# Wider gate tiles in the first unit, a shifted PSUM ring and an earlier request for x

## The chip, the core and the metric

The kernel runs on one core of a Trainium2 chip. The metric is the device time of one execution in microseconds (us). A second source of numbers is one profiled execution, taken by the hardware profiler, whose instructions, waits and transfers are listed with their times from the start of its span.

Names used below: **PE** is TensorE and runs matmuls; **PEld** is its loading of weights, which the profile lists apart; **DVE** is VectorE, **ACT** ScalarE, **POOL** GpSimd; **SP** is SyncE, which here issues transfers. PSUM is the memory that PE writes; the kernel cuts it into four buffers of two banks each. "L541" is line 541 of the kernel.

## The reference

Two stages follow each other. The first is a causal convolution over 7 tokens with softmaxed weights, one set per head (8 heads of 24 channels). The second is a gated feed-forward layer with a ReLU gate.

```python
# x: 8 x 4096 x 192 fp32, weight: 8 x 7
w = softmax(weight)                                   # per head, over the 7 taps
out = einsum('hk,bskhg->bshg', w, windows_of_7(x))    # causal, padded with zeros
x = out.reshape(32768, 192)
gate = maximum(x @ w_gate, 0)                         # w_gate, w_val: 192 x 1536
val  = x @ w_val
return (gate * val) @ w_out                           # w_out: 1536 x 192
```

## The kernel before

**Units.** The 32768 tokens are worked in 16 units (`for u in range(NUNIT)`, L642). A unit is 1024 tokens of each of two streams: the lower and the upper 64 partitions of every tile hold two different halves of the batch. The 192 channels are three chunks `c` of 64 rows. So the convolved input `xc[u]` is a tile of 128 partitions x 3 chunks x 1024 tokens, and `Wg` and `Wv` hold the gate's and the value's weights twice, once for each half of the partitions.

**Gate and value** (`gate_val`, L524). A unit has two windows `w` of 512 tokens, and each window 12 slices `f` of 128 hidden columns. For every slice PE fills two PSUM tiles, `pss[0]` (gate) and `pss[1]` (value). A *step* is one weight matrix and one chunk: four matmuls of 64 x 64 weights over 512 tokens, for the two column halves `q` and the two streams `st` (L541). Six steps make a slice. Behind them ACT takes the ReLU of the gate out of PSUM into `gr` (L551), and DVE multiplies `gr` by the value out of PSUM into `hT` (L552). A gate tile comes free behind L551, a value tile behind L552.

**Projection.** After both windows, `project_turn` (L555) multiplies `hT` by `Wo` in six runs of 48 matmuls (three parts `p`, two turns, L562). Between the turns of a part ACT reads one column (`between_turns`, L575), and at its end DVE transposes the result (L580), which SP stores. The last unit projects in another form (`project`, L605).

**The PSUM ring.** All PSUM tiles come from one pool of four buffers, handed out in the order of the calls of `psum.tile`, round and round. A tile can be written when the tile that had its buffer four calls ago has been read.

**The convolution** is done in three ways. The first window of unit 0 (group 0) and its second (group 1) are *dense pieces* on PE: `conv_steps` (L326) issues 40 small matmuls for each chunk, 118 rows x up to 32 columns of weights over up to 112 tokens (L340). Those of group 1 stand inside the gate of unit 0, ahead of slice 10 of window 0 (`CONV1`, L528): three PSUM tiles, 120 matmuls and three evictions by ACT (L351). Unit 1's input comes from `conv(2)` and `conv(3)` (L353): 8 matmuls each (L363), five moves by ACT (L376) and five transposing transfers that SP issues (L395). `conv(2)` stands behind the gate of unit 0, `conv(3)` behind the first run of its projection. All later units go a *lane*: POOL loads and regroups x (`lane_load`, `lane_turn`, L409 and L446), SP issues eight transposing transfers into `x_r` (L448), ACT starts sums (L494) and makes products (L474), DVE multiplies and adds (L505, L515), POOL adds (L483). The lane of unit u+2 is worked during unit u.

**Order of the work.** It is written out by hand (`manual_schedule`): each engine runs its instructions in the order of the calls. ACT's order behind the gate of unit 0 is: moves of `conv(2)`, the lane's first sums of unit 2 (L494), column of part 0, moves of `conv(3)`, products, and so on up to the first ReLU of unit 1. POOL's order in unit 0 is: requests for x of the lane (L635) and of group 2 (`load_x(2)`, L636), the request for `w_out` (L639), `lane_turn(2)`, the regrouping of `w_out` into `Wo` (L655, two copies), and then the four requests of `load_x(3)` (L656), which bring the x that `conv(3)` reads.

Of the kernel before, what the change touches and what calls it, by code (L numbers as in the profile page):

```python
# [8 lines left out]
FP = mybir.dt.float32  # L9
# [6 lines left out]
def kernel(  # L16
# [12 lines left out]
    nc = tc.nc  # L29
# [40 lines left out]
    psum = ctx.enter_context(tc.tile_pool(name="psum", bufs=4, space=bass.MemoryType.PSUM))  # L70
# [5 lines left out]
    def staged(i, j):  # L76
        return stages[i][:, XH * j : XH * (j + 1)]

    def load_x(g, streams=range(2)):


        bp, toks = GROUPS[g]
        xt = staged(g // 3, g % 3).rearrange("p (j s d) -> p j s d", s=2, d=D)
        for st in streams:
            b = bp + NB * st
            last = toks[-1] == S - SUB or toks[-1] - toks[-2] != SUB
            n_full = len(toks) - int(last)
            lo = toks[0] - PAD
            src = bass.AP(
                tensor=x.tensor,  # L90
                offset=x.offset + (b * S + lo) * D,
                ap=[[D, 128], [SUB * D, n_full], [1, D]],
            )
            nc.gpsimd.dma_start(out=xt[:, 0:n_full, st, :], in_=src)
            if last:
                nc.gpsimd.dma_start(
                    out=xt[0 : SUB + PAD, len(toks) - 1, st, :],
                    in_=x[b, toks[-1] - PAD : toks[-1] + SUB, :],
                )
        return xt  # L100

    xts = {0: staged(0, 0).rearrange("p (j s d) -> p j s d", s=2, d=D)}
# [59 lines left out]
    with nc.allow_low_precision("one of the terms is not zero"):  # L162
        nc.vector.tensor_reduce(
            out=Z[:, 112 : 112 + HR],
# [5 lines left out]
        out=mask[:, :, 0],  # L170
# [26 lines left out]
    for half in range(2):  # L197
        nc.tensor.matmul(
            out=raised[half][:, 0, 0 : SUB * H // 2],
            lhsT=zeros[:],  # L200
# [28 lines left out]
    for s in range(5):  # L229
# [8 lines left out]
        out=mx[:], in_=spread[:, 0, 0:KW], axis=mybir.AxisListType.X, op=ALU.max, negate=True  # L238
# [8 lines left out]
        out=prod[:],  # L247
# [11 lines left out]
        out=blocks[:],  # L259
# [11 lines left out]
    for half, copy in enumerate((nc.vector.tensor_copy, nc.scalar.copy)):  # L271
        for j in range(128 // HR):
# [3 lines left out]
                out=raised[half][:, 0, 0 : SUB * H // 2].rearrange("p (h t) -> p h t", t=SUB)[  # L276
                    :, :, s0 + lo : s0 + hi
                ],
                lhsT=Z[:, 112 - HR * j : 240 - HR * j],
# [5 lines left out]
        for lo, hi in ((0, 3), (3, 4)) if half == 0 else ((0, 4),):  # L285
            copy(  # L286
                out=bands[half][:, lo:hi, :].rearrange("p h t -> p (h t)"),
# [8 lines left out]
    for c in range(NCH):  # L296
        r0 = 0
        while r0 < 64:
# [3 lines left out]
            for st in range(2):  # L302
                nc.sync.dma_start(
                    out=tap[64 * st + r0 : 64 * st + r1, c, :],
# [21 lines left out]
    def conv_steps(g, ps, c, steps):  # L326


        for jj in steps:
            col = SUB * jj  # L330
            n = min(SUB, WIN - col)
            rows = n + PAD
            for second in range(2):
                for st in range(2):
                    for k2 in range(2):
                        k = 2 * c + k2
                        h0, h1 = 32 * k // G, (32 * k + 31) // G
                        h, m = (h0, G * h1 - 32 * k) if second else (h1, 32)
                        p0 = 64 * st + 32 * k2
                        nc.tensor.matmul(  # L340
                            out=ps[p0 : p0 + m, 0, col : col + n],
                            lhsT=xts[g][0:rows, jj, st, 32 * k : 32 * k + m],
                            rhs=band(h)[0:rows, 0:n],
                            start=True,
                            stop=True,
                            tile_position=(0, p0),
                            skip_group_check=True,
                        )

    def evict(copy, g, ps, c):  # L350
        copy(out=xc[0][:, c, WIN * g : WIN * (g + 1)], in_=ps[:, 0, :])  # L351
# [129 lines left out]
    def add(u, k):  # L481
        p0 = prods[u, 0]
        nc.gpsimd.tensor_tensor(  # L483
            out=p0[:] if k < KW - 1 else flat(u)[:, LDVE:FLAT],
            in0=p0[:],
            in1=prods.pop((u, k))[:],
            op=ALU.add,
        )
# [35 lines left out]
    def gate_val(u, w):  # L524
        h = hpool.tile([128, NFF, 2, WIN], F16, name="hT")
        xcb = xc[u]
        for f in range(NFF):
            if u == 0 and w == 0 and f == CONV1:  # L528
                for c in range(NCH):
                    ps = psum.tile([128, 2, 512], FP, name="ps")  # L530
                    conv_steps(1, ps, c, range(GSUB))
                    evict(nc.scalar.copy, 1, ps, c)
            pss = [psum.tile([128, 2, 512], FP, name="ps") for _ in range(2)]
            order = [(i, c) for i in range(2) for c in range(NCH)]
            if u == 0 and w == 0 and f == 0:
                order.insert(1, order.pop(3))
            for i, c in order:
                W = (Wg, Wv)[i]
                for q in range(0, 128, 64):
                    for st in range(2):  # L540
                        nc.tensor.matmul(  # L541
                            out=pss[i][q : q + 64, st, :],
                            lhsT=W[64 * st : 64 * st + 64, c, 128 * f + q : 128 * f + q + 64],
                            rhs=xcb[64 * st : 64 * st + 64, c, WIN * w : WIN * (w + 1)],
                            start=(c == 0),
                            stop=(c == NCH - 1),
                            tile_position=(64 * st, q),
                            skip_group_check=True,
                        )
            gr = gpool.tile([128, 2, WIN], F16, name="gr")  # L550
            nc.scalar.activation(out=gr[:], in_=pss[0][:], func=ACTF.Relu)  # L551
            nc.vector.tensor_tensor(out=h[:, f], in0=gr[:], in1=pss[1][:], op=ALU.mult)  # L552
        return h
# [20 lines left out]
    def between_turns(ps):  # L574
        nc.scalar.copy(out=turned_by[:], in_=ps[:, :, 0])  # L575
# [55 lines left out]
    for c, copy in enumerate((nc.scalar.copy, nc.vector.tensor_copy, nc.scalar.copy)):  # L631
# [8 lines left out]
        out=plain.rearrange("p (c d) -> p c d", d=D), in_=moe_w_out.rearrange("(c p) d -> p c d", p=128)  # L640
    )
    for u in range(NUNIT):  # L642
        lane = 1 <= u < NUNIT - 1
        if lane:
            add(u + 1, 1)
        if u == 1:
            lane_load(3)
            add(2, 2)
            add(2, 3)
        if u + 2 < NUNIT:  # L650
            lane_turn(u + 2)
        if u == 0:
            wide = plain.rearrange("k (f a p d) -> k f a p d", a=2, p=3, d=32)
            for a in range(2):
                nc.gpsimd.tensor_copy(out=Wo[:, :, :, 32 * a : 32 * a + 32], in_=wide[:, :, a, :, :])  # L655
            xts[3] = load_x(3)  # L656
        if 0 < u < NUNIT - 3:
            lane_load(u + 3)
        if lane:
            for k in range(4 if u == 1 else 2, KW - 1):  # L660
                add(u + 1, k)
        hs = [gate_val(u, w) for w in range(2)]
        if lane:
            add(u + 1, KW - 1)
        if u == 0:
            xc[1] = xcpool.tile([128, NCH, UNIT], F16, name="xc")
            conv(2)
        del xc[u]
        bp, w0 = u * UNIT // S, u * UNIT % S // WIN
        lane = None  # L670
        if u + 2 < NUNIT:
            lane_first(u + 2)
            lane = lane_rest(u + 2)
        o = opool.tile([128, UNIT // 64, D], FP, name="out_s")
        if u == NUNIT - 1:
            for i in range(4):
                project(bp, w0 + i // 2, hs[i // 2], i % 2, i == 3, o[:, 4 * i : 4 * i + 4, :])
            continue
        tiles = [None] * 3
        for p, turn in ((0, 0), (1, 0), (0, 1), (2, 0), (1, 1), (2, 1)):  # L680
            if turn == 0:
                tiles[p] = psum.tile([128, 2, 512], FP, name="ps")
            project_turn(hs, p, tiles[p], turn)
            if turn == 0:
                between_turns(tiles[p])
                if u == 0 and p == 0:
                    conv(3)
                if lane:
                    for k in TAPS[p]:
                        product(u + 2, k)  # L690
                if u == 0 and p == 1:
                    psum.tile([128, 2, 512], FP, name="ps")
                continue
            if lane:
                for _ in range(STEPS[p]):
                    next(lane)
            turn_out(tiles[p], o, p)
        store(o, bp, w0)
# [30 lines left out]
```

## Time and profile before

| | us |
|---|---|
| median of 3 runs | 767.27 (767.25 to 768.73) |
| the profiled execution | 766.13 |
| its span, first to last instruction | 764.3 |
| PE busy in the span | 758.3 (99%) |
| DVE busy | 671.0 (88%) |
| ACT busy | 604.2 (79%) |
| POOL busy | 426.5 (56%) |
| matmuls, and as many weight loads | 14011 |
| granted TensorE clock | 1.000 |

The span is what the trace covers; 1.8 us of the execution's own time lie around it. "Busy" of PE is modelled, since matmuls overlap: a matmul is listed with its whole passage through the array, and the next has begun long before that ends. A row of the groups names line, engine, operation, what is written and read, the tile in the array (rows*columns) and the shape, with the count; then the busy time and the mean of one, then the idle time ahead of them and what ended most of it. A row of the timeline starts with its start and its length; in brackets stands the idle time ahead of it. "issue" as a releaser means that the engine waited for nothing that the profile shows.

### The profile page before, as it was taken

The page shows a single profiled execution, that of the slowest core. Times are in us where ns is not written, and L with a number is a line of the kernel's source. Part 1 is how long each engine was busy: PE and PEld are TensorE (multiplying, and loading weights), DVE is VectorE, ACT ScalarE, POOL GpSimd, SP SyncE. Part 2 cuts the span into 40 slices and gives each one's busy share as a digit, 9 for nine tenths or more (in the row PEclk, how much of TensorE's full clock was granted, in tenths as well). Part 3 has the DMA queues.
Part 4 walks back from the last instruction along what each step waited for, and adds up shares of the span by engine and source line. Part 5 has one row for each costly group of instructions (what it writes and reads, how often), then busy time and mean ns, then how long its engine had stood idle before and what let it go on. Part 6 is the DMA issues. An engine that isn't in the chain of part 4 may idle for free.

```text
span 764.3 us, 30954 instructions
## 1 busy us (share of the span) xinstructions
PE 758.3 (99%) x14011; PEld 498.5 (65%) x14011; DVE 671.0 (88%) x631; ACT 604.2 (79%) x667; POOL 426.5 (56%) x192
## 2 busy tenths in 40 slices
PE   9999999999999999999999999999999999999998
PEld 5556666666666666666666666666666666666668
DVE  7779999999899989989899899998999989996691
ACT  6798787878878788787888878878797887874471
POOL 8507839186490955919368292773919549092000
PEclk9999999999999999999999999999999999999999
DMA  9968829093390914709066190842909232040402
GB/s 137 133 80 134 91 42 128 3 135 35 67 102 3 147 22 80 90 8 161 3 104 66 29 142 3 120 50 52 118 3 143 27 75 54 3 84 3 86 3 83
DMA packets 154931, 54.39 MB, mean 71 GB/s; under 512 B 150048, under 2 KB 154800, under 8 KB 154800
## 3 DMA queue, kind: packets, MB, share of 16 engines
q1 hardware_dynamic: 117872, 38.07, 31.8%
q0 software_dynamic: 36768, 14.26, 17.5%
q8 instruction: 109, 1.79, 1.0%
q14 instruction: 22, 0.18, 0.1%
q10 hardware_dynamic: 160, 0.10, 0.0%
HBM read 29.40 MB, written 25.17 MB: 71 GB/s over the span
## 4 chain that ended last, share of the span: by engine, by line
PE 98%; DMA 1%; ACT 0%; issue 0%; SPq 0%
PE ps L541 65%; PE ps L562 31%; PE ps L605 2%; DMA prod<-in_x_dram 1%; PE ps L340 0%; PE ps L363 0%; SPq L111 0%; ACT xc L351 0%; ACT out_s L121 0%; ACT band L286 0%; ACT out_s L616 0%
## 5 line engine op out<-in xcount | busy, mean ns | idle before, releaser
L552 DVE TENSOR_TENSOR hT<-gr,ps 128x1024 f16<-128x1024 f16 x384 | 468.9, 1221 | 36.8 <-ACT gr L551 9.6
L551 ACT ACTIVATE gr<-ps 128x1024 f16<-128x1024 f32 x384 | 393.2, 1024 | 117.5 <-PE ps L541 117.4
L483 POOL TENSOR_TENSOR prod<-prod,prod 128x1792 f32<-128x1792 f32 x70 | 279.8, 3998 | 249.5 <-DVE prod L515 222.8
L541 PE MATMUL ps<-xc,Wg 64*64 64x512 f16 x4608 | 324.6, 376 | 0.6 <-issue 0.5
L541 PE MATMUL ps<-xc,Wv 64*64 64x512 f16 x4608 | 324.1, 376 | 0.0
L562 PE MATMUL ps<-hT,Wo 64*64 64x512 f16 x4320 | 236.3, 376 | 0.0
L541 PEld LDWEIGHTS <-Wg 64*64 64x64 f16 x4608 | 164.5, 107 | 85.3 <-issue 1.7
L541 PEld LDWEIGHTS <-Wv 64*64 64x64 f16 x4608 | 157.7, 106 | 90.9 <-issue 0.3
L562 PEld LDWEIGHTS <-Wo 64*64 64x64 f16 x4320 | 153.9, 107 | 79.0 <-issue 0.3
L474 ACT ACTIVATE prod<-x_r,tap 128x1024 f32<-128x1024 f16 (+1 forms) x182 | 175.1, 1046 | 0.0
L505 DVE SCALAR_TENSOR_TENSOR acc<-x_r,tap,acc 128x1024 f32<-128x1024 f16 (+1 forms) x140 | 113.3, 876 | 2.8 <-ACT acc L494 2.8
L580 DVE STREAM_TRANSPOSE out_s<-ps 128x1024 f32<-128x1024 f32 x45 | 56.2, 1248 | 32.4 <-PE ps L562 28.8
L483 POOL TENSOR_TENSOR xc<-prod,prod 128x1792 f16<-128x1792 f32 x14 | 56.0, 3998 | 1.1
L446 POOL COPY x_p<-x_e 128x1536 f16<-128x1536 f16 x28 | 40.5, 1479 | 0.6 <-DMA x_e<-in_x_dram 0.6
L409 POOL DMA_DIRECT2D x_e<-in_x_dram x28 | 25.0, 898 | 4.2 <-POOL x_p L446 4.2
L505 DVE SCALAR_TENSOR_TENSOR xc<-x_r,tap,acc 128x1024 f16<-128x1024 f16 (+1 forms) x28 | 24.1, 862 | 0.0
L575 ACT COPY turned_by<-ps 128x2 f32<-128x2 f32 x45 | 7.0, 156 | 21.0 <-PE ps L562 19.1
L494 ACT ACTIVATE acc<-x_r,tap 128x1024 f32<-128x1024 f16 (+1 forms) x28 | 21.6, 820 | 0.8 <-DMA x_r<-x_p 0.6
L605 PEld LDWEIGHTS <-hT 128*128 128x128 f16 x192 | 15.8, 98 | 0.4 <-issue 0.4
L605 PE MATMUL ps<-Wo,hT 128*128 128x192 f16 x192 | 16.0, 246 | 0.0
L616 ACT COPY out_s<-ps 128x768 f32<-128x768 f32 (+2 forms) x5 | 3.2, 639 | 12.7 <-PE ps L605 12.7
L616 DVE COPY out_s<-ps 128x192 f32<-128x192 f32 x1 | 0.4, 357 | 13.3 <-PE ps L605 13.3
(57 smaller groups left out, 72.7 us busy)
## 6 DMA issues: line engine op xcount, KB each, us to landing
out_dram<-out_s SPq DMA_DIRECT2D x121, 192.0 KB
x_e<-in_x_dram POOLq DMA_DIRECT2D x28, 384.0 KB, 8.2
x_r<-x_p SPq DMA_TRANSPOSE x112
out_dram<-out_s SPq DMA_DIRECT2D x3, 384.0 KB
out_s<-in_x_dram POOLq DMA_DIRECT2D x4, 240.0 KB, 8.3
prod<-in_x_dram SPq DMA_DIRECT2D x3, 192.0 KB
prod<-in_moe_w_out_dram POOLq DMA_DIRECT2D x1, 576.0 KB, 12.5
out_s<-in_x_dram POOLq DMA_DIRECT2D x2, 192.0 KB, 4.3
```

The lines of the kernel that those rows point to most:

```text
L409: nc.gpsimd.dma_start(out=xe[:, :, st, :, :].rearrange("p j c r -> p j (c r)"), in_=bass.AP(tensor=x.tensor, offset=x.offset + row * D, ap ...
L446: nc.gpsimd.tensor_copy(out=xp[:, :, :, st, :], in_=xe[:, :, st, :, :])
L474: nc.scalar.activation(out=prods[u, k][:, at - LDVE : at - LDVE + n], in_=shifted(u, c, k, t, n), func=ACTF.Copy, scale=tap[:, c, k : k + 1],)
L483: nc.gpsimd.tensor_tensor(out=p0[:] if k < KW - 1 else flat(u)[:, LDVE:FLAT], in0=p0[:], in1=prods.pop((u, k))[:], op=ALU.add,)
L494: nc.scalar.activation(out=accs[u][:, at : at + n], in_=shifted(u, c, 0, t, n), func=ACTF.Copy, scale=tap[:, c, 0:1],)
L505: nc.vector.scalar_tensor_tensor(out=(flat(u) if k == KW - 1 else acc)[:, at : at + n], in0=shifted(u, c, k, t, n), scalar=tap[:, c, k : k ...
L541: nc.tensor.matmul(out=pss[i][q : q + 64, st, :], lhsT=W[64 * st : 64 * st + 64, c, 128 * f + q : 128 * f + q + 64], rhs=xcb[64 * st : 64 ...
L551: nc.scalar.activation(out=gr[:], in_=pss[0][:], func=ACTF.Relu)
L552: nc.vector.tensor_tensor(out=h[:, f], in0=gr[:], in1=pss[1][:], op=ALU.mult)
L562: nc.tensor.matmul(out=ps[64 * st : 64 * st + 64, b, :], lhsT=Wo[64 * r : 64 * r + 64, f, p, :], rhs=hs[b][64 * r : 64 * r + 64, f, st, :] ...
L580: nc.vector.transpose(out=o[:].rearrange("p t (b d) -> p b t d", b=2)[:, :, :, 32 * p : 32 * p + 32], in_=ps[:].rearrange("p b (t c) -> p ...
L605: nc.tensor.matmul(out=ps[:, i // 2, D * (i % 2) : D * (i % 2) + D], lhsT=h[:, f, st, 128 * q : 128 * (q + 1)], rhs=Wo[:, f, :, :].rearran ...
```

## The change

In unit 0 a step of the gate or value takes two matmuls instead of four: 64 rows x 128 columns of weights for each stream, over the same 512 tokens, into the same PSUM tiles. Units 1 to 15 keep 64 x 64. Behind the dense pieces of group 1 one more PSUM tile, `passed`, is taken and one of its columns is set to zero by DVE; nothing reads it. The call of `load_x(3)` stands ahead of the regrouping of `Wo` instead of behind it.

```diff
@@ gate_val
                     conv_steps(1, ps, c, range(GSUB))
                     evict(nc.scalar.copy, 1, ps, c)
+                passed = psum.tile([128, 2, 512], FP, name="ps")
+                nc.vector.memset(passed[:, 0, 0:1], 0.0)
             pss = [psum.tile([128, 2, 512], FP, name="ps") for _ in range(2)]
...
+            M = 64 if u else 128
             for i, c in order:
                 W = (Wg, Wv)[i]
-                for q in range(0, 128, 64):
+                for q in range(0, 128, M):
                     for st in range(2):
                         nc.tensor.matmul(
-                            out=pss[i][q : q + 64, st, :],
-                            lhsT=W[64 * st : 64 * st + 64, c, 128 * f + q : 128 * f + q + 64],
+                            out=pss[i][q : q + M, st, :],
+                            lhsT=W[64 * st : 64 * st + 64, c, 128 * f + q : 128 * f + q + M],
                             rhs=xcb[64 * st : 64 * st + 64, c, WIN * w : WIN * (w + 1)],
@@ for u in range(NUNIT)
         if u == 0:
+            xts[3] = load_x(3)
             wide = plain.rearrange("k (f a p d) -> k f a p d", a=2, p=3, d=32)
             for a in range(2):
                 nc.gpsimd.tensor_copy(out=Wo[:, :, :, 32 * a : 32 * a + 32], in_=wide[:, :, a, :, :])
-            xts[3] = load_x(3)
```

## The prediction, made before the changed kernel was run

> **What bounds the kernel now.** The chain of work that ended last comes first, for it says whose time counts; then the group of matmuls that fills it.
>
> ```profile
> PE 98%; DMA 1%; ACT 0%; issue 0%; SPq 0%
> ...
> L541 PE MATMUL ps<-xc,Wg 64*64 64x512 f16 x4608 | 324.6, 376 | 0.6 <-issue 0.5
> ```
>
> PE is the chain. In the middle units the chain in order of time shows 576 matmuls of L541 in 31.08 us, 54 ns each, although one lasts 376: four run side by side, and a step of four takes 216 ns. That is 0.42 ns for each of its 512 columns of moving data. The last stage (L605, 128 x 192) gives 16.0 us / 192 = 83 ns for 192 columns, 0.43 ns each. So steps stream at the rate of their columns. A gain can only come from places where PE stands still, and the chain shows those in unit 0:
>
> ```profile
> 13.25 9.04 PE ps L541 x164
> 22.29 1.23 PE ps L340 x92
> 23.52 0.67 issue
> 24.18 0.48 PE ps L340 x21
> 24.66 5.52 PE ps L541 x100
> 30.18 0.47 issue
> 30.65 12.93 PE ps L541 x236
> ```
>
> The timeline of weight loads shows the same places sharper, each load being an event of its own:
>
> ```profile
> 13.24 0.14 PEld L541 LDWEIGHTS <-Wg 64*64 64x64 f16 x8 [0.57 <-issue]
> ...
> 22.22 1.13 PEld L340 LDWEIGHTS <-out_s 118*32 118x32 f16 x92 [0.41 <-issue]
> 24.18 0.35 PEld L340 LDWEIGHTS <-out_s 118*16 118x16 f16 x28 [0.83 <-issue]
> ...
> 30.65 0.14 PEld L541 LDWEIGHTS <-Wg 64*64 64x64 f16 x8 [0.95 <-issue]
> ```
>
> Three waits (13.24, 24.18, 30.65) stand in the middle of a step, behind no work that the profile shows. I count PE's pairs of load and matmul up to each: 147 ahead of the gate (3+2+3+2+16+1+120), then 76, 332 and 460 more: 223, 479, 607. The distances are 256 and 128 pairs, and 128 pairs are 256 instructions. The instruction queue moved 1.79 MB in 109 packets, 16.4 KB each, and PE's 28022 instructions are 109.5 times 256. In narrow windows its packets lie at 10.9, 14.3, 21.7, 28.1, 31.7 and 37.5; the waits end 2.3, 2.5 and 2.5 us behind the first, third and fourth. So I read them as **waits for instructions**: crossing into a block sets off the request for the next, its packet follows in about 1 us (13.24 to 14.3) or, when POOL's x loads fill the transfer engines (152 to 164% busy at 22 to 29 us), in 3.9 (24.18 to 28.1), and it is usable some 2.4 us later. A block lasts 6.9 us in the gate, which hides the shorter case, but the dense pieces burn 120 pairs in 1.5 us.
>
> [...] The spacing and the packets speak for the blocks.
>
> **What the waits cost PE.** A half slice (three steps) takes 0.65 us. First wait: from 12.75 to 13.70 instead of 0.65, loss 0.30. Second: the loads of the dense pieces stand 0.83 us, and those resume at full rate, loss 0.83. Third: 29.80 to 31.11, 1.31 instead of 0.65, loss 0.66. Sum **1.79 us**.
>
> **Edit 1, 64 x 128 tiles in unit 0.** 24 slices x 6 steps x 2 = 288 matmuls and as many loads fall away; 144 steps stay. If a step still takes 216 ns, nothing else changes in the stream, but a block now lasts 13.8 us of gate. The new crossings: pair 223 is now gate pair 76, in slice 6, at 12.75 + 3 x 1.295 + 0.22 = 16.85 (its block was usable at 13.25). Pair 351 falls 84 pairs into the dense pieces, which start at 21.92: 21.92 + 84 x 12.3 ns = 22.95. Its request of 16.85 is usable by 20.3 with a delay of 1 us and by 23.15 with 3.9; the one packet requested in a load of this strength (20.2 to 21.7) took 1.5. Pair 479 comes at 33.4, requested at 22.95, usable by 29.3. So the three losses go, and at most 0.2 us is left at the second.
>
> Price of a step: the trace has no 64 x 128 form. Below nothing is excluded, as no form streams a column in under 0.42 ns. At the other end stands a load that nothing hides: L605's 128 x 128 loads last 98 ns, those of L363 (118 x 112) 126 to 130. At 98 to 130 ns for each of 144 steps that is +14.1 to +18.7 us. I take 0, by the nearest row in width:
>
> ```profile
> L605 PEld LDWEIGHTS <-hT 128*128 128x128 f16 x192 | 15.8, 98 | 0.4 <-issue 0.4
> L605 PE MATMUL ps<-Wo,hT 128*128 128x192 f16 x192 | 16.0, 246 | 0.0
> ```
>
> Here loads of 98 ns on all rows hide wholly beneath a stream of 83 ns each; a step of unit 0 has 216. [...] Changes of array shape stay as many as before (gate to dense pieces costs 21.47 to 22.22, 0.10 above 0.65), price 0, at most 0.1 each way for each of four.
>
> **Edit 2, one PSUM tile more.** One memset of one column, 0.06 us by the same form at L136, on DVE behind the product of slice 9, where DVE then stands idle 2.57 us. Nothing waits for it but the value of slice 11, 1.6 us later. Without it slice 10's gate would take the buffer that DVE's product of slice 9 reads until 23.97 (0.30 earlier now: 23.67), while the dense pieces now end at 23.46: a wait of 0.2 us. With it, that gate takes the buffer of the first dense chunk, which ACT leaves at about 23.2. So its cost is 0, and it keeps 0.2 of the 1.79; that is inside the sum.
>
> **Edit 3, the earlier request.** It moves four requests on POOL's queue past the regrouping:
>
> ```profile
> 34.32 2.23 POOL L655 COPY Wo<-prod 128x1152 f16<-128x1152 f16 x2 [3.71 <-DMA prod<-in_moe_w_out_dram]
> 36.50 0.76 POOL L94 DMA_DIRECT2D out_s<-in_x_dram  x1
> 37.24 0.57 POOL L96 DMA_DIRECT2D out_s<-in_x_dram  x1
> 37.80 0.76 POOL L94 DMA_DIRECT2D out_s<-in_x_dram  x1
> 38.55 0.55 POOL L96 DMA_DIRECT2D out_s<-in_x_dram  x1
> ```
>
> They are 2.64 us long and fit into the 3.71 us in which POOL waits for `w_out`, so `Wo` is still ready near 36.6; PE needs it at 42.7, and 6 us of delay would be free. What this moves is traffic. SP's eight transposing transfers for unit 2's lane are issued from 30.64 to 43.04; their last packets lie at 45.4, behind the x load's packets of 37.9 to 43.2. In unit 1, without such a load at the end, the same eight last 12.34 us (79.83 to 92.17), their packets end at 93.0, and ACT, waiting for them, starts at 93.48: 1.31 us behind the issue. This decides what comes next.
>
> ```profile
> 44.17 2.00 ACT L376 CAST out_s<-ps 112x480 f16<-112x480 f32 x5 [0.16 <-PE ps L363]
> 46.35 1.55 ACT L494 ACTIVATE acc<-x_r,tap 128x1024 f32<-128x1024 f16 x2 [0.18 <-issue]
> ```
>
> ACT is the tight engine from here to unit 1: busy 100% from 50 to 60 us, its first ReLU of unit 1 starts at 62.10, about when PE has filled the tile, and PE's value of slice 2 follows the product of that ReLU without slack (64.41 to 64.44). So a gain lasts only if ACT's chain moves too. With PE 1.79 earlier, L494 wants to start at 44.56; `x_r` is usable at 43.04 + 1.31 = 44.35 if the load is out of the way. It fits by 0.2 us. Behind that ACT, DVE, POOL and SP take their start from PE or ACT, and the offset stays to the end.
>
> **Sum.** -1.79 + 0 + 0 = -1.79: execution 766.13 to 764.34, span 764.3 to 762.5. The median of the runs lies 1.14 above the profiled execution; taken along, it goes from 767.27 to 765.48. I say **765.5**, 0.23% faster.
>
> **Rivals.**
> - *The lane eats it.* If `x_r` lands as late as now (45.4 + 0.45 = 45.85, the 0.45 from unit 1), L494 gains 0.5 us instead of 1.79, then all behind it: 766.8. For it: the transfers share the engines whatever their order. Against: unit 1's issue overlaps a larger load at its start and ends no later. 0.13.
> - *The waits are not for instructions.* Then they stay: 767.1 to 767.3. For it: nothing names the queue. Against: the spacing. 0.08.
> - *Slower: the wide load shows.* Two loads of 128 columns in a step are not hidden behind its stream. Place: 144 steps of unit 0. It decides from 1.79 us / 144 = 12.4 ns a step; a whole load gives 767.27 - 1.79 + 14.1 to 18.7 = 779.6 to 784.2. For it: the form is in no row. Against: L605. 0.12.
> - *More goes.* PE also loses 0.20 at 12.11, where slice 2 waits for DVE's first product; nothing here shortens that, but small slacks elsewhere could add to 765.0 or less. 0.05.
>
> The forecast has 0.62. A measurement of this kernel tells about 0.2%, 1.5 us, from no change. The forecast lies 0.26 us beyond that, and with an uncertainty of some 0.3 us in the three losses about four fifths of it count as faster: 0.50 + 0.05 = 0.55. Within 0.2%: 0.12 + 0.13 + 0.08 = 0.33. Slower: 0.12. The range takes in the lane and the waits that stay, and leaves out the wide load (0.12) and little below: 764.8 to 767.4.
>
> **What would show it.** A group of 288 loads 64*128 in unit 0, half slices 0.65 us apart; no "issue" waits of 0.5 us or more among the weight loads between 12 and 32 us; some two instruction packets fewer than 109; `conv(2)` at about 41.7 instead of 43.51; L494 at about 44.6 with little wait for `x_r`; unit 1's gate at about 59.5 instead of 61.2. Half slices above 0.68 us in unit 0, a wait near 23 us, or L494 behind a wait for `x_r` would make it wrong.

## The result, and the profile after

The changed kernel takes 764.53 us (median of 5 runs, 764.42 to 765.63); the kernel before took 768.73 us in the runs beside it (5 runs, 767.25 to 771.66). The ratio is 0.9947, with a 95% interval of 0.9922 to 0.9972: about 4.1 us faster. The forecast was 765.5, 1.8 us faster, within 764.8 to 767.4: the result lies just below that range.

The profiled executions tell another tale than the medians: 766.13 us before and 764.42 after, 1.71 apart, where the prediction had 1.79. So the trace did what was worked out from it. What was mis-sized is how that one execution stands to all the others. In the changed kernel the lines of the gate and the projection lie three further down (one where edit 2 is left out): L544 is the L541 of before, L554 the L551, L565 the L562.

First the chain that ended last, of the changed kernel: its shares, and three of its pieces in order of time (start, length, what).

```profile
PE 99%; DMA 1%; SPq 0%; DVE 0%; issue 0%; ACT 0%
```

```profile
8.73 13.34 PE ps L544 x120
...
23.59 18.28 PE ps L544 x168
...
42.83 2.71 PE ps L565 x48
```

Ten slices run in one piece, 13.34 us, then the dense pieces, then fourteen slices in 18.28. The two "issue" pieces of before are gone. The weight loads at the place of the former second wait:

```profile
21.04 0.55 PEld L544 LDWEIGHTS <-Wv 64*128 64x128 f16 x6
22.00 1.45 PEld L340 LDWEIGHTS <-out_s 118*32 118x32 f16 x120 [0.42 <-issue]
23.52 0.33 PEld L544 LDWEIGHTS <-Wg 64*128 64x128 f16 x6
```

All 120 loads of the dense pieces stand in one row of 1.45 us, where the kernel before had 92, a gap of 0.83 us, and 28. The groups of the new form (busy and mean ns of one, idle ahead of them) and the instruction queue (packets, MB):

```profile
L544 PE MATMUL ps<-xc,Wg 64*128 64x512 f16 x144 | 19.9, 376 | 0.0
...
L544 PEld LDWEIGHTS <-Wg 64*128 64x128 f16 x144 | 7.7, 94 | 7.9 <-issue 0.2
```

```profile
q8 instruction: 107, 1.75, 1.0%
```

A wide matmul lasts 376 ns as a narrow one did, and half slices start 0.65 us apart. Two packets of instructions fewer were fetched; in unit 0 they start at 11.3, 17.9, 26.7, 35.4 and 44.2 us. Last ACT and POOL around the moved request:

```profile
31.17 0.55 POOL L96 DMA_DIRECT2D out_s<-in_x_dram  x1
32.31 2.24 POOL L659 COPY Wo<-prod 128x1152 f16<-128x1152 f16 x2 [0.59 <-DMA prod<-in_moe_w_out_dram]
```

```profile
42.45 2.00 ACT L376 CAST out_s<-ps 112x480 f16<-112x480 f32 x5 [0.17 <-PE ps L363]
44.31 1.58 ACT L494 ACTIVATE acc<-x_r,tap 128x1024 f32<-128x1024 f16 x2
```

The requests fill POOL's wait for `w_out`, of which 0.59 us is left, and L494 starts at 44.31 without a wait for `x_r`. `conv(2)` starts at 41.80 (forecast 41.7) and unit 1's gate at 59.57 (forecast 59.5).

### The profile page after: what moved, and what is told of

Same layout as the page of the kernel before. It is cut to its first block, busy times and chain, and to the rows that moved or that the text cites. A ratio compares the mean times of both kernels' runs of the same rounds, so it can differ in the third digit from the quotient of the medians.

```text
span 762.6 us, 30379 instructions
## 1 busy us (share of the span) xinstructions
PE 758.2 (99%) x13723; PEld 499.6 (66%) x13723; DVE 671.0 (88%) x632; ACT 604.4 (79%) x667; POOL 425.7 (56%) x192
## 4 chain that ended last, share of the span: by engine, by line
PE 99%; DMA 1%; SPq 0%; DVE 0%; issue 0%; ACT 0%
PE ps L544 65%; PE ps L565 31%; PE ps L608 2%; DMA prod<-in_x_dram 1%; PE ps L340 0%; PE ps L363 0%; SPq L111 0%; DVE out_s L121 0%; ACT out_s L619 0%
## 5 line engine op out<-in xcount | busy, mean ns | idle before, releaser
L554 ACT ACTIVATE gr<-ps 128x1024 f16<-128x1024 f32 x384 | 393.3, 1024 | 116.4 <-PE ps L544 116.2
L544 PE MATMUL ps<-xc,Wg 64*64 64x512 f16 (+1 forms) x4464 | 324.3, 376 | 0.0
L544 PE MATMUL ps<-xc,Wv 64*64 64x512 f16 (+1 forms) x4464 | 324.3, 376 | 0.0
L565 PE MATMUL ps<-hT,Wo 64*64 64x512 f16 x4320 | 236.3, 376 | 0.0
L544 PEld LDWEIGHTS <-Wg 64*64 64x64 f16 (+1 forms) x4464 | 164.2, 107 | 84.5 <-issue 0.2
L544 PEld LDWEIGHTS <-Wv 64*64 64x64 f16 (+1 forms) x4464 | 157.5, 106 | 91.2 <-POOL Wg L223 0.3
L565 PEld LDWEIGHTS <-Wo 64*64 64x64 f16 x4320 | 154.7, 107 | 78.2 <-issue 0.3
L494 ACT ACTIVATE acc<-x_r,tap 128x1024 f32<-128x1024 f16 (+1 forms) x28 | 21.6, 822 | 0.5 <-DMA x_r<-x_p 0.5
```

The lines of the kernel that those rows point to most:

```text
L494: nc.scalar.activation(out=accs[u][:, at : at + n], in_=shifted(u, c, 0, t, n), func=ACTF.Copy, scale=tap[:, c, 0:1],)
L544: nc.tensor.matmul(out=pss[i][q : q + M, st, :], lhsT=W[64 * st : 64 * st + 64, c, 128 * f + q : 128 * f + q + M], rhs=xcb[64 * st : 64 * ...
L565: nc.tensor.matmul(out=ps[64 * st : 64 * st + 64, b, :], lhsT=Wo[64 * r : 64 * r + 64, f, p, :], rhs=hs[b][64 * r : 64 * r + 64, f, st, :] ...
```

## The experiments

Two theories were put against each other. **A**: the waits of PE in unit 0 are waits for blocks of instructions; they differ from run to run with the transfers in flight, and wide tiles take them away. **B**: the waits have another cause, or the gain comes from the other two edits.

**The kernel before, again** (no edit):

> The kernel before, unchanged, against itself, for the spread of its times and one more trace. Theory A (the three waits of PE in unit 0 are waits for instruction blocks, and their length varies from run to run with the transfers in flight): runs spread by 2 us or more, 766 to 771, and this trace again shows waits among the weight loads 76, 332 and 460 pairs behind the start of the gate, of other lengths than 0.57, 0.83 and 0.95 us. Theory B (the waits have another cause, and the spread is noise of the measurement): the three waits have the same lengths to 0.1 us, and the spread has no counterpart in the trace.

Its 12 runs went from 765.95 to 771.27 (median 768.45), and 23 runs of the kernel before beside them from 765.39 to 771.62 (median 768.89); the ratio is 1.0001 (0.9983 to 1.0019). So the spread belongs to the kernel. The profiled execution, of 765.95 us, was again one of the fastest. In its trace the wait at pair 223 is missing, the second is 0.83 us as before and the third 0.68 instead of 0.95. Two of the three waits changed in length, and the places of those that are there are those counted.

**Edit 1 alone:**

```diff
+            M = 64 if u else 128
-                for q in range(0, 128, 64):
+                for q in range(0, 128, M):
...
```

> Edit 1 alone: 64 x 128 tiles in unit 0, no extra PSUM tile, load_x(3) behind the regrouping. Theory A: the waits are gone and conv(2) starts at 41.9 to 42.1 (0.2 us behind the changed kernel, by the wait for DVE ahead of slice 10); L494 then waits up to 1.3 us for x_r if the load of x still lies across it, so 764.6 to 766. Theory B (the gain comes from the other two edits): 766 to 769, as before.

Measured: 765.57 (5 runs, 764.34 to 766.12), ratio 0.9946 (0.9927 to 0.9965). No wait for instructions, `conv(2)` at 42.91 in an execution whose gate began 0.93 us later than that of the changed kernel (9.66 against 8.73, for a later x), which covers the 0.8 us by which `conv(2)` missed the expectation, and L494 without a wait for `x_r`. Edit 1 carries the gain.

**Edits 2 and 3 alone:**

```diff
-            M = 64 if u else 128
+            M = 64
```

> Edits 2 and 3 alone: 64 x 64 tiles everywhere, with the extra PSUM tile and the early load_x(3). Theory A: the waits at pairs 223, 479 and 607 stay, so 766 to 769 as before, within 0.5 us of it. Theory B: close to the changed kernel, 764.5 to 765.6.

Measured: 768.52 (12 runs, 766.57 to 771.66), ratio 0.9991 (0.9977 to 1.0006), as the kernel before. B's second half falls. The trace of an execution of 768.17 us shows longer waits at the same two places, among the weight loads:

```profile
14.35 0.14 PEld L544 LDWEIGHTS <-Wg 64*64 64x64 f16 x8 [1.52 <-issue]
...
26.71 0.35 PEld L340 LDWEIGHTS <-out_s 118*16 118x16 f16 x28 [2.25 <-issue]
```

**Without the early request** (edits 1 and 2):

```diff
-            xts[3] = load_x(3)
             wide = plain.rearrange("k (f a p d) -> k f a p d", a=2, p=3, d=32)
...
+            xts[3] = load_x(3)
```

> Edits 1 and 2, without the early load_x(3). By the prediction's rival of the lane: the last packets of x_r lie behind the x load, L494 waits 0.5 to 1.3 us for them and the time is 765.0 to 765.9. If x_r lands in time without edit 3, L494 does not wait, and the time is that of the changed kernel, 764.4 to 764.8.

Measured: 765.19 (5 runs, 764.53 to 766.35), ratio 0.9946 (0.9925 to 0.9967).

```profile
44.67 1.55 ACT L494 ACTIVATE acc<-x_r,tap 128x1024 f32<-128x1024 f16 x2 [0.20 <-issue]
```

The last packets of `x_r` lie before 43.75, with the x load ahead of them as in the kernel before, where they lay at 45.4. L494 was held by them all the same, for a little. Four semaphore instructions of ACT stand ahead of it, and the view of line L494 shows when they ran, here and in the changed kernel:

```profile
L494 ACTq EVENT_SEMAPHORE  x4: 17/38/38, 44.4 to 44.6; - x4
...
L494 ACTq EVENT_SEMAPHORE  x4: 17/38/38, 42.9 to 43.1; - x4
```

In the changed kernel they are done during ACT's moves of `conv(2)`. Here the first ran at 44.38, when the last transfer of `x_r` was signalled (44.36), so that the four reach beyond the end of the moves (44.48) and L494 starts 0.36 us later than in the changed kernel (44.31). The kernel before shows the same: signalled at 46.03, the four at 46.1 to 46.3, and 0.18 us idle. The expectation had 0.5 to 1.3 us or none. It cost PE nothing in this execution: unit 1's gate starts at 59.60, 17.78 us behind `conv(2)` (17.77 in the changed kernel). How often the lane costs more can't be said from one trace, but the times show no sign of it.

**The dose: 64 x 32 tiles in unit 0**, twice the instructions of the kernel before at the same streaming time:

```diff
-            M = 64 if u else 128
+            M = 64 if u else 32
```

> The changed kernel with 64 x 32 tiles in unit 0: eight matmuls a step, 1152 in the gate of unit 0, the same streaming time if eight run side by side in 216 ns. Theory A (instruction blocks): a block of 128 pairs now lasts 3.45 us of gate, and takes 3.4 us to come in quiet stretches and up to 6.3 under POOL's loads; waits of 2 to 3 us at pairs 223, 479, 607 and 735 add up to 9 to 12 us, so 773 to 777. Theory B (the waits hang on the place and not on the number of instructions): at most the waits of the kernel before, 764.5 to 769.

Measured: 779.88 (4 runs, 777.91 to 781.94), ratio 1.0146 (1.0116 to 1.0176). Three rows of its PE timeline:

```profile
13.52 0.83 PE L544 MATMUL ps<-xc,Wv 64*32 64x512 f16 x20 [1.41 <-issue]
...
27.75 1.11 PE L544 MATMUL ps<-xc,Wv 64*32 64x512 f16 x20 [2.93 <-issue]
...
37.69 0.40 PE L544 MATMUL ps<-xc,Wg 64*32 64x512 f16 x4 [2.02 <-issue]
```

Counted in gate and dense pairs, the loads stand still at 76, 204, 332, 460, 588 and 716, that is at every 128th pair, for 1.91, 0.31, 0.68, 3.23, 0.94 and 2.52 us. In undisturbed stretches half slices start 0.65 us apart as always. B falls. A was right that waits stand at the ends of blocks, and short in the size by 3 to 7 us. Of the four places that it named, two had long waits (1.91 at pair 223 and 3.23 at 607), the others 0.68 and 0.94, and a long one stood at pair 863, which it did not name; together the six are 9.6 us, within its 9 to 12. What it left out is the clock: behind the two longest waits the granted clock was 0.50 for 3.41 us each (28.16 to 31.57 and 38.40 to 41.81), and half slices took 1.28 us for a while (39.60 to 40.88). The packets bear out the block as well: 114 for the 29174 instructions of PE here, and 73 for 18806 in the next run, one for every 256 in both.

**Wide tiles in all units:**

```diff
-            M = 64 if u else 128
+            M = 128
```

> The changed kernel with 64 x 128 tiles in all units. If a wide step streams as a narrow one, only two changes of array shape a unit are added, about 0.1 us each, in 15 units: +3 us, 767 to 768.5. If wide steps cost more in the long run, more than that: 144 steps a unit, 15 units, so 1 ns a step is 2.2 us. If changes of shape cost nothing: 764.5.

Measured: 767.61 (12 runs, 767.19 to 769.76), about 2.7 us above the changed kernel beside it. Its chain:

```profile
59.48 31.19 PE ps L544 x288
90.67 15.66 PE ps L565 x288
```

The changed kernel has 31.14 and 15.54 there, and 31.08 or 31.09 in most later units. So 144 wide steps and the two changes of shape around them cost 0.11 + 0.12 us a unit, some 3.3 in all. That it is the changes of shape is the likely reading, and no run tells the two apart; the time behind `conv(2)` is 3.1 longer than in the first execution of the changed kernel (725.68 against 722.62). The price of a wide step itself is thus below 0.11 us / 144, under 1 ns.

**The changed kernel, again:**

> The changed kernel again, for the spread of its times beside the kernel before on one chip. Theory A: 764.4 to 766.4, a spread of less than half that of the kernel before (765.4 to 771.6), and no wait above 0.45 us among the weight loads of the gate of unit 0.

Measured: 764.89 (7 runs, 764.46 to 766.25), ratio 0.9954 (0.9936 to 0.9971), a spread of 1.8 us against 4.6 for the kernel before beside it (18 runs, 766.53 to 771.09). No wait for instructions in its trace of unit 0. As expected.

**Without the extra PSUM tile** (edits 1 and 3):

```diff
-                passed = psum.tile([128, 2, 512], FP, name="ps")
-                nc.vector.memset(passed[:, 0, 0:1], 0.0)
```

> The changed kernel without the extra PSUM tile (edits 1 and 3). By the prediction PE waits 0.2 us for DVE's product of slice 9 ahead of slice 10, and the time is 0.2 us longer than the changed kernel's, 764.6 to 766.6; the wait shows in the trace, the time alone can't tell it.

Measured: 764.88 (6 runs, 764.63 to 765.59), ratio 0.9952 (0.9933 to 0.9970). PE's first row behind the dense pieces:

```profile
24.39 0.82 PE L542 MATMUL ps<-xc,Wg 64*128 64x512 f16 x6 [0.20 <-DVE hT L553]
```

The wait is there, 0.20 us by the trace; the times cannot tell it.

**Dense pieces one slice later**, on the kernel before:

```diff
-    CONV1 = 10
+    CONV1 = 11
```

> The kernel before (64 x 64 everywhere) with the dense pieces ahead of slice 11 instead of slice 10. Theory A, by counting blocks: the same 256 instructions end at other places. Pair 479 now falls 68 pairs into the dense pieces and comes about 1.1 us later, so its wait (0.8 and 2.3 us so far) gets shorter or goes; pair 607 stands only 76 gate pairs, 2.0 us, behind the dense pieces, against a block that takes 3.4 to 6.3 us from its request: a wait of 1.5 to 3.6 us some 2 us behind the dense pieces. Time 767 to 771. Theory B (the waits belong to the dense pieces or to a moment of the run): the wait stays inside the dense pieces or at 30 us, as long as before.

Measured: 768.03 (10 runs, 766.71 to 768.79), ratio 0.9990 (0.9978 to 1.0002). Its weight loads:

```profile
24.03 0.88 PEld L340 LDWEIGHTS <-out_s 118*32 118x32 f16 x68 [0.41 <-issue]
26.40 0.61 PEld L340 LDWEIGHTS <-out_s 118*8 118x8 f16 x52 [1.49 <-issue]
32.59 0.14 PEld L541 LDWEIGHTS <-Wg 64*64 64x64 f16 x8 [1.71 <-issue]
```

The waits moved exactly as counted: behind 68 dense pairs instead of 92 (264 + 68 = 332), and behind 76 gate pairs instead of 100. The third became longer, 1.71, as A had it. The second did not shrink: its packet came at 23.9, 3.2 us behind its crossing at 20.7 instead of the 1.5 of the trace that I had reckoned with, and was usable some 2.5 us later.

**Loads out of the way**, on the kernel before: the requests for `w_out` and for x of groups 2 and 3 behind `lane_turn(2)`:

```diff
-    xts[2] = load_x(2)
-    nc.gpsimd.dma_start(out=plain..., in_=moe_w_out...)
...
             lane_turn(u + 2)
         if u == 0:
+            nc.gpsimd.dma_start(out=plain..., in_=moe_w_out...)
+            xts[2] = load_x(2)
+            xts[3] = load_x(3)
...
-            xts[3] = load_x(3)
```

> The kernel before (64 x 64 everywhere) with POOL's requests for w_out and for x of groups 2 and 3 behind lane_turn(2), so that hardly any load is in flight from some 24 to 30 us, where the block of pair 607 is fetched. Theory A: that block's packet follows its request by about 1 us instead of 3.9, the third wait (0.5 to 0.95) goes, the first two stay; 0.5 to 1.5 us less than the kernel before, if Wo is regrouped in time for the projection (w_out lands at 35 to 38, needed at 43). Theory B: the three waits stay.

Measured: 769.85 (10 runs, 767.90 to 772.70), ratio 1.0018 (1.0000 to 1.0037): not faster. PE's rows with a wait:

```profile
24.77 0.48 PE L340 MATMUL ps<-band,out_s 118*16 118x112 f16 x28 [1.22 <-issue]
...
44.36 1.00 PE L363 MATMUL ps<-out_s,band 118*112 118x240 f16 x8 [0.86 <-DMA out_s<-in_x_dram]
...
50.80 1.82 PE L363 MATMUL ps<-out_s,band 118*112 118x240 f16 x8 [2.73 <-DMA out_s<-in_x_dram]
```

The mechanism came out: between 24 and 28 us the transfer engines are busy 46% instead of some 160, the packet follows the crossing of 24.77 by about 1 us (25.9), and no third wait is left; the first two stayed, the second at 1.22 us. But x of groups 2 and 3 now came too late for `conv(2)` and `conv(3)`, 3.6 us of new waits, and behind the longer, of 2.73 us, the granted clock was 0.50 for 6.83 us. The size of the forecast failed through the remedy.

**Two more traces of the kernel before:**

> The kernel before, one more trace. Theory A: the execution's time is 763.0 to 764.3 us (its time without waits) plus what the waits at pairs 223, 479 and 607 cost PE in this trace, to 0.7 us.

> The kernel before, one more trace. Theory A: as for the run ahead of it, the execution's time is 763.0 to 764.3 us plus what the waits at pairs 223, 479 and 607 cost PE in this trace, to 0.7 us.

They were executions of 770.99 and 769.15 us. Weight loads of the second:

```profile
14.34 0.14 PEld L541 LDWEIGHTS <-Wg 64*64 64x64 f16 x8 [0.91 <-issue]
...
26.46 0.35 PEld L340 LDWEIGHTS <-out_s 118*16 118x16 f16 x28 [2.01 <-issue]
32.93 0.14 PEld L541 LDWEIGHTS <-Wg 64*64 64x64 f16 x8 [0.95 <-issue]
```

The first has a wait of 3.37 us in the dense pieces, and behind it a lower clock; its windows from 24 to 32 us show it (behind the busy times of PE, PEld, DVE, ACT and POOL stand PEclk, the transfers' share and GB/s; 0.57 is a mean, the clock was 0.50 from 28.11 to 31.52):

```profile
27.48 0.35 PEld L340 LDWEIGHTS <-out_s 118*16 118x16 f16 x28 [3.37 <-issue]
```

```profile
24.00:28.00 4.00, 0.80 (x59) 0.58 (x48) 0.73 (x1) 0.76 (x2) 0.02 (x1) 1.00 1.63 190
28.00:32.00 4.00, 4.00 (x48) 1.83 (x48) 1.22 (x1) 1.85 (x3) 3.42 (x4) 0.57 0.97 120
```

The traces of the kernel before, of the changed kernel and of the versions that leave out one or two of its edits, cut at the first gate matmul and at `conv(2)`, in us:

| execution | gate starts | from there to `conv(2)` | the rest | time |
|---|---|---|---|---|
| before, shown first | 8.59 | 34.92 | 722.62 | 766.13 |
| before again | 8.43 | 34.68 | 722.84 | 765.95 |
| edits 2 and 3 alone | 8.78 | 36.66 | 722.73 | 768.17 |
| before, second of two more | 9.38 | 36.41 | 723.36 | 769.15 |
| before, first of two more | 9.58 | 38.25 | 723.16 | 770.99 |
| changed | 8.73 | 33.07 | 722.62 | 764.42 |
| changed again | 8.78 | 33.10 | 723.01 | 764.89 |
| without the early request | 8.79 | 33.03 | 722.71 | 764.53 |
| without the extra tile | 9.31 | 33.31 | 722.80 | 765.42 |
| edit 1 alone | 9.66 | 33.25 | 723.09 | 766.00 |

"The rest" is the time less the first two, with what lies around the span. It spreads alike for narrow (722.62 to 723.36) and wide tiles (722.62 to 723.09). The middle column is 33.0 to 33.3 with wide tiles whatever the execution, and 34.7 to 38.3 with narrow ones: 1.6 to 5.2 us of waits, in the longest together with the lower clock behind it. The last two expectations missed by 0.8 us: without the waits both executions would stand at 765.8, above the base of 763.0 to 764.3 with its 0.7, since their gate starts 0.8 to 1.0 us later and their rest is 0.5 to 0.7 us longer. The wide kernels show the same reach without any such wait (764.3 to 766.4).

No version beat the changed kernel; the three that leave out edit 2, edit 3 or both can't be told from it by their times.

## Why the prediction was right and wrong, point by point

- **What bounds the kernel, and the three waits**: right. Blocks of 256 instructions are shown by the places of the waits in the dose (at every 128th pair) and in the shifted dense pieces (behind 68 dense pairs instead of 92, behind 76 gate pairs instead of 100), by one packet for every 256 instructions in kernels of 18806 to 29174 (73 to 114 packets), and by the packet that came faster once the loads were out of the way (about 1 us behind its crossing instead of 3.9).
- **Edit 1's price of 0**: right. Wide steps stream at 216 ns (half slices of three start 0.65 us apart), and 2160 of them in later units bound any surplus below 1 ns each. The rival of the slower wide load is out: with the matmuls of both streams running throughout, loads of 94 ns stay hidden.
- **The new crossings**: right, with a slip that nothing hangs on. Pair 76 lies two wide steps into slice 6 and not one, so the first crossing is at 12.75 + 3.885 + 0.43 = 17.07 and not at 16.85. The packets at 17.9 and 26.7 follow the crossings of 17.07 and 22.95 by 0.8 and 3.7 us, and no wait is left in the dense pieces.
- **Sum for the one execution**: right, 764.34 forecast and 764.42 measured, span 762.5 and 762.6. That it agrees to 0.1 us is partly luck: this execution had its gate's start (8.73 against 8.59) and its rest (722.62 in both) almost as the kernel before; other wide executions have up to 0.9 and 0.5 us more there.
- **"The median of the runs lies 1.14 above the profiled execution; taken along"**: this is the step that failed. The 1.14 us were not an offset around every execution but for the most part more of the very waits that the change removes: the changed kernel's median lies only 0.11 above its profiled execution. The traces measure the loss at 1.6 to 5.2 us, with the trace that I had at 1.85 near the lower end; from median to median it is 768.7 to 764.5, 4.1 to 4.2 us. The term "what the waits cost PE" was 1.79 and should have been about 4 for the median, and the median of three runs that it was taken from (767.27) was itself low, 768.73 beside the changed kernel. The range fell with the same term: its lower end of 764.8 allowed for little more than the waits of one trace. The shown runs had a sign of it (767.25 to 768.73 against a profiled 766.13), and the prediction itself said that a fetch takes 1 or 3.9 us by the load of transfers, which is to say that it varies.
- **Edit 2**: right in mechanism and size, 0.20 us in the trace without it; the times cannot tell it.
- **Edit 3**: right that it costs nothing and that `Wo` is in time. Its worth was put too high: in the trace that lacks edit 3 alone the last packets of `x_r` came before 43.75, not at 45.4, and L494 started 0.36 us later, with no loss for PE; with edit 1 alone it did not wait. The 1.29 us of the rival of the lane have no case in any trace here. The prediction also missed that L494's 0.18 us "issue" in the kernel before was already the end of a wait for `x_r`.

## What to carry to other kernels

An engine that stands still "for issue" in the middle of a step may be out of instructions: count them between such waits, and see whether the distances are multiples of one number (256 here) and whether packets of the instruction queue precede the ends by a fixed time (2.3 to 2.5 us here). Doing the same work in fewer, larger instructions helped here where blocks were used up faster than they came; that was unit 0 alone (1.6 to 5.2 us of waits with narrow tiles, none for instructions with wide ones), and in the later units the wide form cost 0.23 us each, most likely for the changes of shape. And a wait that hangs on contention is not one number (the one in the dense pieces took 0.83 to 3.37 us): before its removal is priced from one trace, the spread of the times should be read as, in good part, the spread of that wait.

## What the hardware showed unexpectedly

- The wait for the same block at the same place took 0.83, 0.83, 2.01, 2.25 and 3.37 us in five executions of narrow tiles, and one kernel's times spread over 6 us.
- Behind long waits of PE the granted clock was low for a few us, but not behind all of them: behind 2.93 and 2.02 us of idle PE (64 x 32 tiles) and 3.20 us (770.99 us execution) it was 0.50 for 3.41 us each, and in the last a slice and a half took 3.65 us instead of 1.94; at the 2.73 us of the loads out of the way it was 0.50 for 6.83 us. Behind 1.85 and 2.09 us in two others it stayed at 1.00.
- The traces show a pattern in this, which no run was made to test. In the 13 traces that list changes of the clock, these lie, within a trace, whole multiples of 3.41 us apart (20.48, 3.41 and 6.83 with the 64 x 32 tiles). Counted in stretches of that length from the first change on, PE idled 2.02, 2.10, 2.79 and 2.93 us in the four stretches behind which the clock fell, and at most 1.41 us in any other at full clock before the last stage. The waits of 1.85 and 2.09 us were cut in two by the end of a stretch (25.77 and 25.62), into 1.16 us at most.
